# Issuing the last two parts of product P6 together in the two w2·h blocks

## The chip, the cores and the metric

The kernel runs on one core of one Trainium2 chip. That core has four compute engines with queues of their own: TensorE (PE in the profile; its weight loads are listed apart as PEld), VectorE (DVE), ScalarE (ACT) and GpSimd (POOL). SyncE (SP) issues most of the DMA transfers. Within one queue the instructions of this kernel stand in a fixed order, and the queues meet through semaphores. The metric is device time in microseconds, the median of three runs.

## What is computed

With x of 2048 rows by 512 columns, the reference is

```python
g = sigmoid((x * gate_w).sum(-1, keepdims=True))
a = Cr @ (x @ Dr.T) - Ci @ (x @ Di.T)      # the real part of a Fourier transform over both axes
b = (silu(x @ w1) * (x @ w3)) @ w2         # 512 -> 1376 -> 512
out = g * a + (1 - g) * b
```

All arrays are float32. Only the product of h = silu(x w1) · (x w3) with w2 is touched by the change.

## The kernel before

Every large product is done as one step of a Strassen-like scheme with seven products of half-size blocks (P1 to P7), and every operand is split into a high and a low part of type fp32r, so that one logical product becomes three matmuls (`mm3`, L122 by way of `matmul`: high·high, high·low, low·high). The right operand is split while the kernel runs: ACT copies the high part (`high`, L108) and DVE subtracts it from the source to get the low part (`low`, L111). The split pair is called `zo`.

After the gate and up projections (the first 206 us) the work is a list `STEPS` of steps, in blocks. Four blocks of kind "F" multiply by the Fourier matrix of the sequence, two blocks of kind "H" (numbers 4 and 5) compute w2·h, and two of kind "Y" finish the transform over the columns. A step is one *part* q of one product k of a block: part q takes a slice of the contraction. In an H block each product has three parts: q = 0 and q = 1 bring 1024 columns of z (two groups of 512, so 2 × 3 = 6 matmuls into each half of the result, 12 in all), and q = 2 brings 512 (3 into each half, 6 in all). The result of a product has two halves, r = 0 and r = 1, of 128 rows each; each has its own PSUM bank, `ps[0]` and `ps[1]`. A matmul takes 128x128 weights and a 128x512 z.

In H blocks the products stand in the order P1, P5, P6, P7, P3, P2, P4. P1, P6, P7 and P4 share the two banks called X: P6 adds onto what P1 left, and P7 adds onto P6. P5 and P3 share the banks Z. Between P6 and P7 the sum in X must be copied out, as `u2` (`zu` in the profile): when P6's last part has been issued, `read("u2")` puts two ACT copies into ACT's queue (L1061), the first of `ps[0]`, the second of `ps[1]`, each 128x512. P7's first matmul writes into `ps[0]` and so has to wait for the first copy.

One step does, in this order of the program: take its split pair `zt` out of `ZT`, issue its matmuls, `free(zt)`, then `advance(m)`, and after the last part of a product the reads of its banks. `advance(m)` prepares the future: it starts loads (`load_c`), forms a sum for the step four ahead (`sum_c`, on DVE), and splits the operand of the step three ahead (`split_c(m + LEAD)`, `LEAD` = 3). So when P6's part 2 is issued, `advance` splits P7's part 2, and its ACT copy stands in ACT's queue *ahead* of the two copies of X. This is the sequence in ACT's queue around the end of P6, in both kernels: split of P7's part 0 (1024 columns), of P7's part 1 (1024), of P7's part 2 (512), then copy of X's first half, copy of X's second half, then the split of P3's part 0.

The split pairs live in four buffers, the list `ZO`. It is a plain queue: `take` pops the first free one, `free` appends to the end.

```python
def take(places, shape, dtype, name):      # L90
    p, tag = at = places.pop(0)
...
def free(*tiles):                          # L102
    for t in tiles:
        _, places, at = HELD.pop(id(t))
        places.append(at)
```

A new tile in a buffer waits until the last reader of the buffer's former tile is done. With four buffers, a lead of three and one pair freed at each step, there is one free buffer ahead of a step; the split in step m takes the buffer that step m − 1 gave back.

The list `LAST` and the test `m >= len(STEPS) - 2` are there already for the very last two steps of the kernel, whose matmuls are issued together.

Of the kernel before, what the change touches and what calls it, by code (L numbers as in the profile page):

```python
# [32 lines left out]
def fnet_swiglu_gate_kernel(  # L33
# [46 lines left out]
    def bank(k, name):  # L80
        return psum.tile([P, 512], F32, tag=f"ps{k}", name=name)
# [17 lines left out]
    def parts(name):  # L99
        return take(ZO, [P, 2, 4, 256], F32R, name)  # L100
# [5 lines that stand above are left out]
# [36 lines left out]
    def flat(ap):  # L142
        return ap.rearrange("p a n -> p (a n)")
# [300 lines left out]
    zt = parts("b12"), parts("a21")  # L444
# [195 lines left out]
    n = NI - 1 - LOOK  # L640
# [23 lines left out]
    NQ = [{"F": NG // 2, "H": NP2 // 2, "Y": KD // 2}[k] for k in KIND]  # L664
    LEFT_AT = "P3", 0
    STEPS = []
# [32 lines left out]
    def cols(blk, q, form):  # L699

        return 512 if KIND[blk] == "H" and q == NQ[blk] - 1 else 1024
# [80 lines left out]
    def advance(m):  # L782
        load_c(m + LEAD + AHEAD)
        sum_c(m + LEAD + 1)
        split_c(m + LEAD)
# [122 lines left out]
    def spill(blk, k, t, ps=None):  # L908

        src = [t[:, r] for r in range(2)] if ps is None else ps
        if KIND[blk] != "Y":
            g = GT[blk][k // 2] if KIND[blk] == "H" else GT[blk][0]
            for r in range(2):
                nc.vector.tensor_mul(t[:, r], src[r], g)
            if KIND[blk] == "F":
                return nc.gpsimd.dma_start(z_rows(blk, k), flat(t))
            return nc.gpsimd.dma_start(out_part(nbsp, 2 * (blk - NTB) + k // 2, k), t)
        nb, o = other.pop((blk, k))  # L920
        b = nb.rearrange("p (r n) -> p r n", r=2)
        if ps is None:
            nc.vector.tensor_add(flat(t), flat(t), nb)
            nc.sync.dma_start(o, t)
        else:
            last = blk == NB - 1
            for r in range(2 - last):
                nc.vector.tensor_add(t[:, r], ps[r], b[:, r])  # L928
                (nc.scalar if r else nc.sync).dma_start(o[:, r], t[:, r])
            if last:  # L930


                nc.vector.tensor_add(t[:, 1, :256], FINAL[1][:, :256], b[:, 1, :256])
                nc.scalar.dma_start(o[:, 1, :256], t[:, 1, :256])
                nc.scalar.activation(t[:, 1, 256:], ps[1][:, 256:], AF.Copy)  # L935
                nc.sync.dma_start(o[:, 1, 256:], t[:, 1, 256:])
        free(nb)

    GT, other, LAST, FINAL = {}, {}, [], {}

    def out_part(v, tb, k):
        rows = slice(k % 2 * 2 * P, (k % 2 + 1) * 2 * P)
# [33 lines left out]
    def left_step(m):  # L976


        blk = STEPS[m][0]
        w, e = STAT["L"], RL.pop((blk, "e"))  # L980
        z = ZT[m].rearrange("p h a n -> p h (a n)")
        U["P2"] = [bank(b, f"P2_{blk}_{r}") for r, b in enumerate(YB)]
        U["L"] = [bank(b, f"L_{blk}_{r}") for r, b in enumerate(XB[1 - blk % 2])]
        into = [(j, g, ps) for j, names in ((1, ("P5", "L")), (0, ("P2", "P1")))
                for g, ps in enumerate(U[names[0]] + U[names[1]])]
        for n in range(2):
            for j, g, ps in into:
                b = 512 * n + (256, 384, 0, 128)[g]
                matmul(ps, w[:, b : b + P], z[:, j, 512 * n : 512 * n + 512],
                       start=n == 0 and (j, g // 2) in ((0, 0), (1, 1)), stop=False,  # L990
                       skip_group_check=True)
        for j, g, ps in into:
            rows = slice(32 * g, 32 * g + 32)
            matmul(ps, w[rows, 8 * P :], e[rows, 512 * j : 512 * j + 512],
                   start=False, stop=(j, g // 2) == (1, 1), skip_group_check=True)
        free(e)

    def step(m):
        blk, q, k, form = STEPS[m]
        kind = KIND[blk]  # L1000
        if k == "L":
            left_step(m)
            free(ZT.pop(m))
            advance(m)
            for r in range(2):
                nc.vector.tensor_add(U["p5"][:, r], U["p5"][:, r], U["L"][r])
            return spill(blk, 3, U["p5"])
        if q == 0 and k == "P6" and kind != "Y":
            load_gate(blk)
        if blk == NB - 1 and k == "P7" and q == 0:  # L1010
            nb = other[blk, RESULT[k]][0]
            nc.vector.tensor_add(flat(U["p5"]), flat(U["p5"]), nb)
            free(nb)
        own = k in ("P1", "P5", "P2") and (k, kind) != ("P2", "H")
        if q == 0 and own:
            banks = {"P1": XB[blk % 2], "P5": ZB, "P2": YB}[k]
            U[k] = [bank(b, f"{k}_{blk}_{r}") for r, b in enumerate(banks)]
        ps = U[{"P6": "P1", "P7": "P1", "P4": "P1", "P3": "P5"}.get(k, k)]
        zt = ZT.pop(m)
        z = zt.rearrange("p h a n -> p h (a n)")  # L1020
        first = k in ("P1", "P5", "P6", "P3")
        ws = STAT[kind][0 if first else 1]
        steps = [(q, z)]
        if m >= len(STEPS) - 2:
            LAST.append((q, z))
            steps = LAST if m == len(STEPS) - 1 else []
        ni = cols(blk, q, form) // 512
        f = FORMS[kind][k]
        final = blk == NB - 1 and k == "P4"
        if final and steps:  # L1030
            FINAL[1] = bank(XB[1 - blk % 2][0], "P4left")

        def banks_of(r):

            if r == 0 or not final:
                return [(ps[r], slice(None), own)]
            return [(FINAL[1][:, :256], slice(0, 128), True), (ps[1][:, 256:], slice(128, 256), False)]

        for r in range(2):
            sl = slice(r * P, (r + 1) * P)  # L1040
            for dst, some, new in banks_of(r) if steps else ():
                for n, zn in steps:
                    for i in range(ni):
                        w = ws[2 * n + i]
                        b = slice(i * 512, (i + 1) * 512)
                        mm3(dst, w[:, 0, f, sl], w[:, 1, f, sl], zn[:, 0, b], zn[:, 1, b],
                            new and n == 0 and i == 0, n == NQ[blk] - 1 and i == ni - 1, not new,
                            some)
        free(zt)
        advance(m)  # L1050
        if q < NQ[blk] - 1:
            return

        def res(name):
            U[name] = ut.tile([P, 2, 512], F32, tag=name, name=f"z{name}_{blk}")
            return U[name]

        def read(name):
            res(name)
            for r in range(2):  # L1060
                nc.scalar.activation(U[name][:, r], ps[r], AF.Copy)  # L1061

        def plus(name):
            for r in range(2):
                nc.vector.tensor_add(U[name][:, r], U[name][:, r], ps[r])

        if k == "P1":
            read("s1")
        elif k == "P5":
            read("p5")  # L1070
        elif k == "P6":
            read("u2")
        elif k == "P3":
            def result():
                plus("u2")
                spill(blk, 2, U["u2"])

            result() if blk else todo.setdefault(m + 3, []).append((result, ()))
        elif k == "P7" and blk == NB - 1:
            o = other.pop((blk, RESULT[k]))[1]  # L1080
            nb = other[blk, RESULT["P4"]][0].rearrange("p (r n) -> p r n", r=2)
            p5, u3 = U["p5"], res("u3")
            nc.scalar.activation(u3[:, 0], ps[0], AF.Copy)
            for r, v in enumerate((u3[:, 0], ps[1])):
                nc.vector.tensor_add(p5[:, r], p5[:, r], v)
                nc.sync.dma_start(o[:, r], p5[:, r])
            nc.vector.tensor_add(nb[:, 1, :256], nb[:, 1, :256], ps[1][:, :256])
            nc.vector.tensor_add(ps[1][:, 256:], ps[1][:, 256:], nb[:, 1, 256:])
        elif k == "P7":
            read("u3")  # L1090
            nc.vector.tensor_add(flat(U["p5"]), flat(U["p5"]), flat(U["u3"]))
            if kind != "H":
                spill(blk, 3, U["p5"])
        elif k == "P2":
            plus("s1")
            spill(blk, 0, U["s1"])
        else:
            spill(blk, 1, res("c21"), ps)
# [23 lines left out]
    for i, (src, sp, p) in enumerate(late):  # L1122
        blk, b = 1 + i // 3, i % 3
        n = (10, 17, 24)[b]
# [97 lines left out]
```

## Time and profile before

| | us |
|---|---|
| median of 3 runs (lowest, highest) | 674.75 (674.49, 674.79) |
| the profiled execution's own time | 674.51 |
| its span in the trace | 672.7 |
| PE busy in the span | 667.9 |
| DVE busy | 597.0 |
| ACT busy | 374.0 |
| end of P6 in block 4, on the trace's time axis | about 516 |
| end of P6 in block 5 | about 566 |

Times in the trace count from the start of the span. In a timeline each row is a run of like instructions: start, length, engine, line, operation, output<-input, the form, the count, and in brackets how long the engine was idle before it and what ended that. Weight loads (PEld) run ahead of the matmul that they belong to, so a wait of TensorE shows at the weight load. `P` is a bank of a product, `zo` a split pair, `H` the weights from w2, `B` a raw operand.

### The profile page before, as it was taken

To read this page: it belongs to the slowest core of one execution; us is meant where nothing else is said; L and a number is where in the kernel's file an instruction comes from. 1 tells how busy PE (TensorE), PEld (TensorE's weight loads), DVE (VectorE), ACT (ScalarE), POOL (GpSimd) and SP (SyncE) were. 2 spreads that over 40 slices of the span, in tenths; PEclk is the share of its full clock that TensorE was granted. 3 is DMA by queue.
4 is the path that set the end of the run, shared out by engine and by line. 5 is a ranking of instruction groups with operands and counts; after the bars stand their busy time and mean duration, and the time that the engine had idled before them with its cause. 6 is when DMAs were issued, how large, how long until landed. Compare 5 with 4: busy or idle time off the path is not lost.

```text
span 672.7 us, 8720 instructions
## 1 busy us (share of the span) xinstructions
PE 667.9 (99%) x3101; PEld 580.2 (86%) x3101; DVE 597.0 (89%) x749; ACT 374.0 (56%) x505; POOL 66.4 (10%) x123
## 2 busy tenths in 40 slices
PE   9999999999999999999999999999999999999998
PEld 6888888888888888888888888888888888888887
DVE  6999988887679999988899899979797797898996
ACT  6775666655447764466454653654445446455451
POOL 0022112221110000001310101100000010000000
PEclk9999999999999999999999999999999999999999
DMA  7576557499998666815776279919986894784942
GB/s 281 206 296 249 224 205 267 187 340 380 405 418 328 234 216 211 308 64 196 275 263 255 81 248 343 386 41 349 341 323 184 288 347 134 286 313 153 342 130 94
DMA packets 46845, 171.37 MB, mean 255 GB/s; under 512 B 5649, under 2 KB 6225, under 8 KB 43089
## 3 DMA queue, kind: packets, MB, share of 16 engines
q1 hardware_dynamic: 33888, 118.18, 49.7%
q0 software_dynamic: 12624, 52.25, 19.8%
q8 instruction: 24, 0.39, 0.2%
q10 hardware_dynamic: 288, 0.39, 0.2%
q14 instruction: 21, 0.16, 0.1%
HBM read 114.88 MB, written 55.91 MB: 254 GB/s over the span
## 4 chain that ended last, share of the span: by engine, by line
PE 98%; DMA 1%; ACT 0%; DVE 0%; SPq 0%; issue 0%
PE P L122 68%; PE X L122 16%; PE Z L122 8%; PE Y L122 4%; PE C L122 2%; DMA xs_B<-xt 1%; DMA out<-zc 0%; PE L L122 0%; DVE zc L928 0%; ACT xo L108 0%; SPq L242 0%; ACT zc L935 0%
## 5 line engine op out<-in xcount | busy, mean ns | idle before, releaser
L122 PE MATMUL P<-zo,a 128*128 128x512 f32 x1344 | 290.3, 379 | 0.0
L122 PEld LDWEIGHTS P<-zo,a 128*128 128x128 f32 x1344 | 253.9, 189 | 36.3 <-DVE zo L111 0.2
L108 ACT ACTIVATE zo<-B 128x1024 fp32r<-128x1024 f32 (+1 forms) x182 | 185.1, 1022 | 178.5 <-PE P L122 81.1
L111 DVE TENSOR_TENSOR zo<-B,zo 128x1024 fp32r<-128x1024 f32 (+1 forms) x182 | 213.1, 1179 | 26.6 <-ACT zo L108 26.1
L122 PE MATMUL P<-zo,H 128*128 128x512 f32 x420 | 91.9, 380 | 0.1
L751 DVE TENSOR_TENSOR B<-B,B 128x1024 f32<-128x1024 f32 (+1 forms) x78 | 91.8, 1177 | 0.1
L122 PEld LDWEIGHTS P<-zo,H 128*128 128x128 f32 x420 | 79.1, 189 | 12.6 <-ACT zu L1061 0.9
L122 PE MATMUL X<-xo,wb 128*128 128x512 f32 x378 | 88.8, 379 | 0.0
L122 PEld LDWEIGHTS X<-xo,wb 128*128 128x128 f32 x378 | 71.3, 189 | 10.4 <-DMA wb<-wbsp 0.3
L122 PE MATMUL P<-zo,Y 128*128 128x512 f32 (+1 forms) x336 | 71.6, 375 | 0.0
L122 PEld LDWEIGHTS P<-zo,Y 128*128 128x128 f32 x336 | 62.7, 189 | 8.7
L348 POOL DMA_DIRECT2D hsp<-h x40 | 21.7, 543 | 101.5 <-DVE h L408 70.6
L122 PE MATMUL X<-xo,wa 128*128 128x512 f32 x126 | 30.6, 379 | 0.0
L122 PE MATMUL Y<-xo,wa 128*128 128x512 f32 x126 | 30.6, 379 | 0.0
L122 PE MATMUL Z<-xo,wb 128*128 128x512 f32 x126 | 30.6, 379 | 0.0
L122 PE MATMUL Z<-xo,wa 128*128 128x512 f32 x126 | 30.6, 379 | 0.0
L755 DVE TENSOR_TENSOR B<-B,B 128x1024 f32<-128x1024 f32 (+1 forms) x26 | 30.6, 1177 | 0.0
L122 PEld LDWEIGHTS X<-xo,wa 128*128 128x128 f32 x126 | 23.8, 189 | 3.4
L122 PEld LDWEIGHTS Y<-xo,wa 128*128 128x128 f32 x126 | 23.8, 189 | 3.4
L122 PEld LDWEIGHTS Z<-xo,wb 128*128 128x128 f32 x126 | 23.8, 189 | 3.4
L122 PEld LDWEIGHTS Z<-xo,wa 128*128 128x128 f32 x126 | 23.8, 189 | 3.4
L111 DVE TENSOR_TENSOR wa<-ws,wa 128x768 fp32r<-128x768 f32 (+1 forms) x22 | 19.3, 880 | 6.6 <-ACT wa L108 6.4
(166 smaller groups left out, 578.0 us busy)
## 6 DMA issues: line engine op xcount, KB each, us to landing
B<-cc SPq DMA_DIRECT2D x64, 512.0 KB, 5.5
hsp<-h POOLq DMA_DIRECT2D x40, 256.0 KB, 4.1
wbsp<-wb POOLq DMA_DIRECT2D x8, 1024.0 KB, 4.2
wb<-wbsp SPq DMA_DIRECT2D x8, 1024.0 KB, 8.1
B<-hsp SPq DMA_DIRECT2D x16, 512.0 KB, 4.9
B<-zsp SPq DMA_DIRECT2D x16, 512.0 KB, 6.9
ws<-w SPq DMA_DIRECT2D x11, 512.0 KB, 4.7
H<-w2sp SPq DMA_DIRECT2D x5, 1024.0 KB, 8.9
```

The lines of the kernel that those rows point to most:

```text
L108: nc.scalar.activation(hi, src, AF.Copy)
L111: nc.vector.tensor_sub(lo, src, hi.bitcast(F32))
L122: nc.tensor.matmul(ps.rearrange("p (n a) -> p n a", a=2), u, turns(v)[:, some], **kw)
L348: nc.gpsimd.dma_start(hsp[g, b + k, j // 2, :, j % 2 * 512 : (j % 2 + 1) * 512], h)
L751: nc.vector.tensor_add(t, t, RAW[blk, b, q][:, :n])
L755: nc.vector.tensor_sub(t, RAW[blk, "B12", q][:, :n], t)
```

## The change

In the two H blocks, the last two parts of P6 (q = 1 and q = 2) are no longer issued one after the other. At part 1 nothing is issued to TensorE; the pair is put into `LAST` and, as `zt`, into the new list `WAITS`, so that its buffer is not given back yet. `advance` is still called. At part 2 the matmuls of both parts are issued: first all that go into X's first half (6 of part 1, 3 of part 2), then all that go into its second half (6 and 3). Then both buffers are given back, part 2's first and part 1's behind it.

```diff
-    GT, other, LAST, FINAL = {}, {}, [], {}
+    GT, other, LAST, WAITS, FINAL = {}, {}, [], [], {}
...
         steps = [(q, z)]
-        if m >= len(STEPS) - 2:
+        together = m >= len(STEPS) - 2 or (kind, k) == ("H", "P6") and q >= NQ[blk] - 2
+        if together:
             LAST.append((q, z))
-            steps = LAST if m == len(STEPS) - 1 else []
-        ni = cols(blk, q, form) // 512
+            steps = LAST if q == NQ[blk] - 1 else []
...
                 for n, zn in steps:
+                    ni = cols(blk, n, form) // 512
                     for i in range(ni):
...
-        free(zt)
+        if steps:
+            free(zt, *WAITS)
+            LAST.clear()
+            WAITS.clear()
+        else:
+            WAITS.append(zt)
         advance(m)
```

The number of matmuls, copies, splits and transfers is unchanged on every engine.

## The prediction

> **What bounds the kernel now.** I read the page first, then TensorE's list of waits, then the timelines of TensorE and ACT around the two ends of P6.
>
> ```profile
> span 672.7 us, 8720 instructions
> ...
> PE 667.9 (99%) x3101; PEld 580.2 (86%) x3101; DVE 597.0 (89%) x749; ACT 374.0 (56%) x505; POOL 66.4 (10%) x123
> ...
> PE 98%; DMA 1%; ACT 0%; DVE 0%; SPq 0%; issue 0%
> ```
>
> TensorE is busy nearly all the time and is 98% of the chain that ended last. So what is lost on TensorE is lost in the whole, and what any other engine loses counts only where TensorE then waits for it.
>
> ```profile
> PEld P L122 <- issue: 1.3, 4, 0.3
> PEld P L122 <- ACT zu L1061: 0.9, 2, 0.4
> ...
> PEld P L122 <- DVE zo L111: 0.2, 1, 0.2
> ```
>
> These are all the waits of TensorE in the blocks (total us, times, longest). The middle row is the place of the change: two waits, one per H block, of P7's first weight load for the ACT copy of X. The other rows are also the whole reserve: a later TensorE cannot win back more than 0.2 us from DVE, and the issue waits are nobody's. The same from close by, for block 4; first TensorE's steps:
>
> ```profile
> 529.89 30.48 PE L122 MATMUL P<-zo,H 128*128 128x512 f32 x140
> 514.61 0.59 PE L122 MATMUL P<-zo,H 128*128 128x512 f32 x2
> 515.25 0.59 PE L122 MATMUL P<-zo,H 128*128 128x512 f32 x2
> 515.90 0.59 PE L122 MATMUL P<-zo,H 128*128 128x512 f32 x2
> 516.54 0.70 PE L122 MATMUL P<-zo,H 128*128 128x512 f32 x2
> 516.53 0.19 PEld L122 LDWEIGHTS P<-zo,H 128*128 128x128 f32 x1 [0.44 <-ACT zu L1061]
> ```
>
> A matmul lasts 0.38 us, so a row of two that covers 0.59 has its second start at start + 0.59 − 0.38. The first row gives the step from one matmul to the next: (30.48 − 0.38) / 139 = 0.2165 us. In the second row the second matmul, at 514.82, is the last of P6's part 1; six of part 2 follow: three into X's first half (last start 515.46), three into its second (last start 516.11). P7's weight load then comes at 516.53 with 0.44 idle before it. Its second matmul starts at 516.54 + 0.70 − 0.38 = 516.86, where without a wait it would be at 516.11 + 2 × 0.2165 = 516.54: the wait costs 0.32 us net, twice, 0.64 us in all. That is everything there is to gain here.
>
> ```profile
> 515.29 0.63 ACT L108 ACTIVATE zo<-B 128x512 fp32r<-128x512 f32 x1 [1.53 <-PE P L122]
> 515.89 0.60 ACT L1061 ACTIVATE zu<-P 128x512 f32<-128x512 f32 x1
> 516.53 0.60 ACT L1061 ACTIVATE zu<-P 128x512 f32<-128x512 f32 x1
> ```
>
> The first row is the split of P7's part 2, ahead of the copies in ACT's queue. It waits for TensorE: its buffer was that of P6's part 1, whose last matmul started at 514.82, so it starts 0.47 later, still beside part 2's matmuls. The first copy starts 0.43 after its own last matmul (515.46), the second 0.42 after its own (516.11). So now the split delays the copy hardly at all.
>
> **The change, part by part.** *The matmuls.* The same 18 of parts 1 and 2 in another order; TensorE has as many steps, cost nothing. Part 2's operand is wanted six steps (1.3 us) earlier. P6's last matmul starts at 516.11 and part 1 begins 17 steps before, at 512.43; with the change part 2 begins six steps later, at 513.73. In block 5 all is 49.92 us later (last start 566.03, below), so 563.65. The low halves of these operands end at 510.28 and 561.26:
>
> ```profile
> 509.59 0.69 DVE L111 TENSOR_TENSOR zo<-B,zo 128x512 fp32r<-128x512 f32 x1
> 560.58 0.68 DVE L111 TENSOR_TENSOR zo<-B,zo 128x512 fp32r<-128x512 f32 x1
> ```
>
> Over 2 us in hand: nothing lost. By itself the new order would do good: X's first half would be complete nine matmuls before the second instead of three, so its copy could run beside them.
>
> *The buffers.* But part 1's pair is no longer given back at part 1, and at part 2 `free(zt, *WAITS)` appends part 2's buffer first, part 1's second. `advance` comes right behind and its split of P7's part 2 pops the first: **the buffer of P6's part 2, whose last reader is now P6's very last matmul**. Before, it was part 1's. Nothing else is free at that point: of four buffers two hold P7's parts 0 and 1. The waits in ACT's queue, read from the two built programs (S is the number of P6's last matmul in TensorE's count):
>
> ```
>              before                     after
> split P7/2   TensorE >= S-6             TensorE >= S
> copy X, 1st  TensorE >= S-3             none of TensorE
> copy X, 2nd  TensorE >= S               none of TensorE
> ```
>
> The copies need no wait of their own any more because they stand behind the split. So in place of "copy beside the second half's matmuls" comes a chain in series: last matmul, split, copy, P7's weight load.
>
> *Its price.* Last matmul to split: 0.47, by the present split. Split to copy: where one 512-wide ACT instruction follows another and waits for nothing, the start to start is 0.53 (522.60 to 523.13):
>
> ```profile
> 519.48 0.63 ACT L733 ACTIVATE zo<-left_a 128x512 fp32r<-128x512 f32 x1 [1.41 <-issue]
> 520.13 0.63 ACT L733 ACTIVATE zo<-left_b 32x512 fp32r<-32x512 f32 x1
> ...
> 522.60 0.63 ACT L733 ACTIVATE left_e<-left_c 128x512 fp32r<-128x512 f32 x1
> 523.13 1.04 ACT L108 ACTIVATE zo<-B 128x1024 fp32r<-128x1024 f32 x1
> 524.08 0.57 ACT L1061 ACTIVATE zu<-P 128x512 f32<-128x512 f32 x1
> 524.08 1.06 ACT L1061 ACTIVATE zu<-P 128x512 f32<-128x512 f32 x2
> ```
>
> Copy to weight load: 516.53 − 515.89 = 0.64. So the load comes at 516.11 + 0.47 + 0.53 + 0.64 = 517.75 instead of 516.53: **1.22 us later**. What follows the wait is as before, so this is the loss. In block 5:
>
> ```profile
> 565.21 0.63 ACT L108 ACTIVATE zo<-B 128x512 fp32r<-128x512 f32 x1 [1.53 <-PE P L122]
> 565.82 0.59 PE L122 MATMUL P<-zo,H 128*128 128x512 f32 x2
> 566.45 0.19 PEld L122 LDWEIGHTS P<-zo,H 128*128 128x128 f32 x1 [0.44 <-ACT zu L1061]
> ```
>
> last matmul 566.03, split at 566.50, copy at 567.03, load at 567.67 against 566.45: 1.22 again. Bounds of one block: 0.42 (a copy's lag behind its matmul), 0.49 (two `zu`, 0.57 the first, 1.06 together) and 0.62 (such a shorter copy, with the same 0.05 from its end to the load) give 1.53 and a loss of 1.11; 0.47, 0.65 (519.48 to 520.13, with a wait for a transfer between) and 0.65 give 1.77 and a loss of 1.35. I take 1.22 since its rows are nearest: same sizes, same line, no other wait.
>
> *The second copy* starts half a microsecond behind the first, at 517.6, and ends at 518.2; P7's first matmul into X's second half comes six steps after the load, at 519.0: covered, by 0.8 us.
>
> *Who else waits.* Behind the split stands DVE's low half of the same operand (now at 515.95, then some 1.3 us later, by 517.9); DVE's queue has nothing else to do then, its next row waits for ACT:
>
> ```profile
> 515.95 0.69 DVE L111 TENSOR_TENSOR zo<-B,zo 128x512 fp32r<-128x512 f32 x1 [0.94 <-ACT zo L108]
> 517.03 1.05 ACT L108 ACTIVATE zo<-B 128x1024 fp32r<-128x1024 f32 x1
> 568.02 1.23 DVE L111 TENSOR_TENSOR zo<-B,zo 128x1024 fp32r<-128x1024 f32 x1 [1.47 <-ACT zo L108]
> ```
>
> P7's part 2 is wanted 24 steps (5.2 us) after P7 begins, near 523: covered. The split of P3's part 0 (517.03) moves to some 518.2, wanted at P7's end, 30 steps after its start. Everything later on ACT and DVE moves with TensorE by the same 1.2 us. SP and POOL issue the same transfers in the same order; those that wait for nothing here come as early as before, which can only help. From the two stalls on, TensorE has no reserve but the 0.2 us named.
>
> *The clock.* Idle time of the weight loads becomes 0.44 + 1.22 = 1.66 us in each block. The nearest stall in the trace is at the head, 1.30, and the granted clock there is full:
>
> ```profile
> core 0: us, PE busy (x) PEld busy (x) DVE busy (x) ACT busy (x) POOL busy (x), PEclk, DMA share, GB/s
> 4.50:6.50 2.00, 1.20 (x6) 0.78 (x5) 1.38 (x3) 1.14 (x3) 0.00 (x0) 1.00 0.98 383
> 0.78 3.85 PE L434 MATMUL wps<-const-bfloat16-1.0 128*128 128x512 bf16 x11 [0.78 <-PEq L1211]
> 5.43 0.30 PEld L122 LDWEIGHTS C<-xo,wa 128*128 128x128 f32 x2 [1.30 <-ACT xo L108]
> ```
>
> So I add nothing for it. [...]
>
> *The sum.* 2 × 1.22 = 2.44 us, bounds 2.22 and 2.70. On the profiled execution's 674.51 that is 676.95; that run lies 0.24 below the median of the three (674.75), on which it would be 677.19. I say **677.1 us**, +0.35%.
>
> **The rivals.** *1. The split does not hold the copies back*, so the order does what the words of the change say. X's first half is then complete nine steps before the end, the copy starts at 516.11 − 9 × 0.2165 + 0.43 = 514.59, ends at 515.2, and the wait is gone: −0.64 us, 674.1 (−0.09%). It decides where the split starts by 516.12 − 0.64 − 0.53 = 514.95, so where its buffer's last reader starts by 514.48, eight matmuls before the last one. For it: the wait of 0.4 is real. Against it: the buffer's reader is the last matmul. Chance 0.04.
>
> *2. The wait is for part 1's matmuls only* (buffer order the other way round). Part 1's last matmul would be three from the end, at 515.46; split 515.93, copy 516.46, load 517.10: 0.57 later, 1.14 in all, 675.8 (+0.16%). For it: before, it was part 1's buffer; against it: `free` appends part 2's first. Chance 0.04.
>
> *3. The clock falls after the longer stalls.* The only slow matmuls of the trace are the eleven at the head, (3.85 − 0.38) / 10 = 0.35 a step. If each stall is followed by eleven such steps, 11 × (0.35 − 0.2165) = 1.5 us more per block: 680.1 (+0.8%). For it: the stall is longer than any in the trace; against it: full clock after 1.30. Chance 0.04.
>
> **How the numbers follow.** Forecast 0.88, rivals 0.04 each. The forecast's own range, bounds of the sum on either base, is 676.7 to 677.45. A measurement of this kernel tells about 0.2% (1.35 us, so 673.4 to 676.1) from no change. Of both signs only rival 1 lies below; more than eight in ten lie with the forecast, so the range is its own with a little for the medians' scatter of 0.3 between runs: 676.5 to 677.6. Slower: forecast and rival 3, 0.92; same: rivals 1 and 2, 0.07 and a bit; faster, 0.01.
>
> **What would show it.** Right: TensorE's waits for `zu` L1061 go from 0.9 to some 3.3 us, still two; ACT's `zo` 128x512 at the end of P6 begins about 0.47 behind P6's last matmul and both `zu` follow it without a gap, the first 0.5 later; TensorE's busy steps keep 0.2165 us. Wrong: a first copy that starts before the last matmul of P6 (rivals 1 and 2), a PEclk digit below 9 in the slices near 516 or 567 (rival 3), or a wait for DVE or a DMA that grows in blocks 5 to 7, which would say that the delay does not shift everything alike.

## The result, and the profile after

| | before | changed |
|---|---|---|
| median, us (6 runs each) | 674.79 (674.49 to 675.07) | 677.24 (676.87 to 677.73) |
| profiled execution, its own time | 674.51 | 677.14 |
| span in the trace | 672.7 | 675.4 |
| waits of TensorE for `zu`, us | 0.9 | 3.3 |

The ratio is 1.0036, with a 95% interval of 1.0023 to 1.0049: slower by 2.45 us. The forecast was 677.1 (676.5 to 677.6).

TensorE's waits in the changed kernel, from its list of waits (weight loads; total us, times, longest; the copy of X now has line 1067):

```profile
PEld P L122 <- ACT zu L1067: 3.3, 2, 1.7
...
PEld P L122 <- issue: 1.3, 4, 0.3
...
PEld P L122 <- DVE zo L111: 0.2, 1, 0.2
```

Still two waits, of 1.66 us each instead of 0.44; the other two rows are what they were. The end of P6 in block 4 of the changed kernel, in the timelines of TensorE and ACT (start us, length us):

```profile
516.01 0.59 PE L122 MATMUL P<-zo,H 128*128 128x512 f32 x2
517.85 0.19 PEld L122 LDWEIGHTS P<-zo,H 128*128 128x128 f32 x1 [1.66 <-ACT zu L1067]
517.86 0.70 PE L122 MATMUL P<-zo,H 128*128 128x512 f32 x2 [1.25 <-ACT zu L1067]
...
516.69 0.63 ACT L108 ACTIVATE zo<-B 128x512 fp32r<-128x512 f32 x1 [2.83 <-PE P L122]
517.22 0.58 ACT L1067 ACTIVATE zu<-P 128x512 f32<-128x512 f32 x1
517.22 1.07 ACT L1067 ACTIVATE zu<-P 128x512 f32<-128x512 f32 x2
```

P6's last matmul starts at 516.01 + 0.59 − 0.38 = 516.22. Then the four links stand one behind the other: the split 0.47 later (516.69), the first copy 0.53 after the split (517.22), the weight load 0.63 after the copy (517.85). The split's bracket says that ACT had been idle for 2.83 us, waiting for TensorE: the copy of X's first half, complete nine steps earlier, stood behind it all that time. In block 5 it is the same:

```profile
567.82 0.63 ACT L108 ACTIVATE zo<-B 128x512 fp32r<-128x512 f32 x1 [2.83 <-PE P L122]
568.36 1.06 ACT L1067 ACTIVATE zu<-P 128x512 f32<-128x512 f32 x2
568.99 0.19 PEld L122 LDWEIGHTS P<-zo,H 128*128 128x128 f32 x1 [1.66 <-ACT zu L1067]
```

Nothing is won back or lost further on. TensorE's busy time by stages, first of the changed kernel, then of the one before (length of the stretch, busy us):

```profile
496.00:530.00 34.00, 32.75 (x152) 28.38 (x151) 24.93 (x27) 19.40 (x27) 0.53 (x1) 1.00 0.71 241
530.00:600.00 70.00, 68.75 (x327) 58.88 (x327) 60.63 (x73) 33.64 (x43) 5.04 (x7) 1.00 0.74 260
600.00:660.00 60.00, 60.00 (x280) 52.55 (x279) 57.03 (x55) 32.65 (x39) 0.72 (x1) 1.00 0.63 223
```

```profile
496.00:530.00 34.00, 33.96 (x162) 28.90 (x162) 25.05 (x28) 20.18 (x28) 0.53 (x1) 1.00 0.76 262
530.00:600.00 70.00, 69.96 (x328) 60.44 (x329) 62.96 (x75) 34.56 (x44) 5.05 (x7) 1.00 0.76 266
600.00:660.00 60.00, 60.00 (x280) 52.54 (x279) 57.05 (x56) 32.45 (x39) 0.72 (x1) 1.00 0.59 210
```

One block's stall lies in each of the first two stretches, 1.2 us of busy time is missing in each, and behind them TensorE is full again, at a granted clock of 1.00 throughout. The spans differ by 2.7, not 2.4: 0.1 is there before block 4 (516.22 against 516.11), in the head of the kernel, and the rest behind the last matmul; neither touches the change.

### The profile page after: what moved, and what is told of

It is laid out like the page before. It is cut to its first block, busy times and chain, and to the rows that moved or that the text cites. A ratio compares the mean times of both kernels' runs of the same rounds, so it can differ in the third digit from the quotient of the medians.

```text
span 675.4 us, 8714 instructions
## 1 busy us (share of the span) xinstructions
PE 668.4 (99%) x3101; PEld 580.7 (86%) x3101; DVE 596.7 (88%) x749; ACT 373.2 (55%) x505; POOL 66.4 (10%) x123
```

## The experiments

Theory: part 2's buffer, given back first, makes the split of P7's part 2 wait for P6's last matmul, and the copies of X are late because they stand behind that split in ACT's queue. Rivals: the new order of the matmuls costs the time by itself; or the late buffer does, wherever the copies stand.

**The hold alone.** The kernel before, its own order of matmuls, with the buffers given back as in the change:

```diff
-    GT, other, LAST, FINAL = {}, {}, [], {}
+    GT, other, LAST, WAITS, FINAL = {}, {}, [], [], {}
...
-        free(zt)
+        if (kind, k) == ("H", "P6") and q == NQ[blk] - 2:
+            WAITS.append(zt)
+        else:
+            free(zt, *WAITS)
+            WAITS.clear()
         advance(m)
```

> The kernel before with its own order of matmuls, but part 1's buffer is given back only after part 2's, as in the change. Theory (the buffer alone makes the loss): the same last matmul, split, copy, load in series, so 677.2, waits for zu 3.3 us. Rival (the order of the matmuls makes it): 674.8, waits 0.9.

Measured 677.13 us (8 runs), ratio 1.0029 (1.0019 to 1.0039) to 674.79. From its list of waits, and from its timelines at the end of P6 in block 4:

```profile
PEld P L122 <- ACT zu L1065: 3.3, 2, 1.7
...
516.67 0.63 ACT L108 ACTIVATE zo<-B 128x512 fp32r<-128x512 f32 x1 [2.83 <-PE P L122]
517.21 1.07 ACT L1065 ACTIVATE zu<-P 128x512 f32<-128x512 f32 x2
...
517.84 3.32 PEld L122 LDWEIGHTS P<-zo,H 128*128 128x128 f32 x16 [1.66 <-ACT zu L1065]
```

It is the same chain, link by link. The whole loss is there without a single matmul moved. What changed the time is not what the change's words speak of, the order of the matmuls, but when and in which order two buffers are given back.

**The other buffer.** The changed kernel with part 1's buffer given back first:

```diff
-            free(zt, *WAITS)
+            free(*WAITS, zt)
```

> The changed kernel, but part 1's buffer is given back ahead of part 2's, so that the split of P7's part 2 takes part 1's buffer and waits for part 1's last matmul, three steps (0.65 us) before P6's end. Theory (the chain last reader, split, copy, weight load sets the wait): the load comes 0.65 us earlier than in the changed kernel in each block, so 1.3 us in all: 677.24 - 1.3 = 675.9, with the waits for zu at about 2.0 us in all instead of 3.3. Rival (the loss comes from the new order of the matmuls, not from the buffer): stays at 677.2.

Measured 675.73 us (12 runs, one of which took 678.53 at a mean granted clock of 1.000), ratio 1.0016 (1.0006 to 1.0026). Its waits and its ACT timeline at the end of P6 in block 4:

```profile
PEld P L122 <- ACT zu L1067: 2.0, 2, 1.0
```

```profile
516.32 0.63 ACT L108 ACTIVATE zo<-B 128x512 fp32r<-128x512 f32 x1 [2.18 <-PE P L122]
516.86 1.06 ACT L1067 ACTIVATE zu<-P 128x512 f32<-128x512 f32 x2
```

The last matmul that the split waits for comes three steps earlier, the split's idle time falls from 2.83 to 2.18, by 0.65 = three steps, and the wait falls with it from 1.66 to 1.01. The wait follows the split's start, step for step. Part 1's last matmul still lies so near P6's end that the copies stay late, so this order too loses time, only less.

**The copies first.** The changed kernel, buffers and matmuls as changed, with the two copies put ahead of the split in ACT's queue:

```diff
-        advance(m)
+        late = (kind, k) == ("H", "P6") and q == NQ[blk] - 1
+        if not late:
+            advance(m)
...
             read("u2")
+            if late:
+                advance(m)
```

> The changed kernel, but at P6's last part the two copies of X are put into ACT's queue ahead of the split of P7's part 2; buffers and matmuls as changed. Theory (the split loses the time only because the copies stand behind it in ACT's queue): the first copy starts nine matmuls before P6's end, TensorE does not wait at all: 674.79 - 0.64 = 674.15, waits for zu 0. Rival (order of the matmuls, or the late buffer itself, costs): 676 to 677.2. Second rival (the late split is then missed by P7's part 2 or by DVE): a wait of TensorE for zo by DVE or ACT of over 0.5 us.

Measured 673.90 us (12 runs), ratio 0.9985 (0.9976 to 0.9993): 0.89 us faster than before and 3.3 faster than the changed kernel. It is the best of all kernels tried. In its list of waits no row for `zu` is left; these are all that TensorE has in the blocks:

```profile
PEld P L122 <- issue: 1.3, 4, 0.3
PEld P L122 <- DVE zo L111: 0.2, 1, 0.2
```

Its ACT timeline at the end of P6 in block 4 (this execution took 676.19 us, the 11 others 673.64 to 674.44; in it TensorE's weight loads at the head came to their full pace late, from 10.55 us on, so all times are some 2 us later; the last section has more on that):

```profile
516.73 0.60 ACT L1069 ACTIVATE zu<-P 128x512 f32<-128x512 f32 x1 [0.83 <-PE P L122]
518.68 0.60 ACT L1069 ACTIVATE zu<-P 128x512 f32<-128x512 f32 x1 [1.35 <-PE P L122]
519.17 1.57 ACT L108 ACTIVATE zo<-B 128x512 fp32r<-128x512 f32 x2
```

The copies are 1.95 us apart, nine steps of 0.2165: each follows its own half at once. The split now comes last, with the same late buffer as in the change, and nobody waits for it. So the late buffer by itself costs nothing that these runs can tell; what costs is that the split which waits for it stands ahead of the copies.

**The copies first, in the kernel before.** The same edit without the new order and without the hold.

> The kernel before, its order of matmuls and its buffers, with only the two copies of X put ahead of the split of P7's part 2. Theory (before, the first copy was bound by its own last matmul, 0.43 behind it, and the split ahead of it cost nothing): the two waits of 0.44 stay, 674.8. Rival (the split ahead of the copies already cost time before the change, so that the gain of 0.9 us with the changed order comes from the queue alone): 673.9, waits gone.

Measured 674.73 us (11 runs) against 674.72, ratio 1.0000 (0.9991 to 1.0009). The wait stands:

```profile
PEld P L122 <- ACT zu L1063: 0.9, 2, 0.4
```

So the gain above needs both: the new order of matmuls, and the copies ahead of the split. The first without the second is the change, a loss; the second without the first gives nothing.

**One block only.** The change in block 4, not in block 5:

```diff
-        together = m >= len(STEPS) - 2 or (kind, k) == ("H", "P6") and q >= NQ[blk] - 2
+        together = m >= len(STEPS) - 2 or (blk, k) == (NTB, "P6") and q >= NQ[blk] - 2
```

> The change in block 4 only. Theory (each block adds its own 1.22 us, nothing given back later): 674.79 + 1.22 = 676.0, one wait for zu of 1.66 and one of 0.44, 2.1 us in all. Rival (a delay in the first block is partly won back, or makes the second worse): under 675.5 or over 676.5.

Measured 676.06 us (12 runs), ratio 1.0018 (1.0007 to 1.0029), waits for `zu` 2.1 us in two, the longest 1.7. Each block pays its own 1.2. One of the 12 runs took 678.69 us, at a mean granted clock of 0.997 where the others have 0.999 or 1.000; no trace of it was kept, and the clock is taken up below.

**More in the chain.** The changed kernel, with ACT's copy of that split done twice:

```diff
             high(t[:, 0, :n], src[:, :n])
+            if KIND[blk] == "H" and (k, q) == ("P7", NQ[blk] - 1):
+                high(t[:, 0, :n], src[:, :n])
```

> The changed kernel, with the ACT copy of the split of P7's part 2 done twice in both H blocks (the same values written again). Theory (what stands in ACT's queue between P6's last matmul and the copy of X is paid in full by TensorE): one more 128x512 copy per block, 0.53 us, or up to 0.75 if the second waits for the first to be written: 677.24 + 1.1 to 1.5 = 678.3 to 678.7, waits for zu 4.4 to 4.8 us. Rival (part of the loss is a fixed cost of the semaphores and the extra copy hides in it): 677.2 to 677.7.

Run beside the changed kernel itself:

> The changed kernel once more, on the same chip as the two others of this set, as their base: 677.2, waits for zu 3.3 us. No theory expects another time.

The changed kernel took 677.60 (5 runs, ratio 1.0042, 1.0029 to 1.0055). With the copy doubled the waits grew from 3.3 to 4.6 us, 0.65 per block and copy, inside what was expected (0.53 by a row, up to 0.75 by an estimate that no run shows), and two of six runs took 678.1 and 678.2. But the median was 680.0 (ratio 1.0072, 1.0060 to 1.0083): the other four took 679.9 to 680.7, at a mean granted clock of 0.997. That was a miss: the median lies 1.3 us above the upper end of what was expected. Two more profiled executions of the same kernel, and a kernel with the copy done four times (a loop of three in place of the `if`), were to tell where the 2 us between the two groups of runs lie:

> The kernel with the split's copy done twice, one more look, to see where the 2 us lie that four of its six runs took above the profiled one (678.1). Theory A: 678.1, or more with slow first matmuls at the head of the kernel. Theory B: near 680, with matmul steps of 0.3 us or more behind the stall in block 4 or 5.

> A second such look at the kernel with the split's copy done twice. Theory A: 678.1, or more with slow first matmuls at the head of the kernel. Theory B: near 680, with matmul steps of 0.3 us or more behind the stall in block 4 or 5.

> The changed kernel with the ACT copy of the split of P7's part 2 done four times in both H blocks (the same values). One extra copy lengthened each of the two waits by 0.65 us. Theory A (the stall alone is paid, 0.65 us per copy and block, and the scatter up to 680.7 in the timed runs with one extra copy comes from the head of the kernel): 677.4 + 6 x 0.65 = 681.3, waits for zu 7.2 us, every matmul after the stalls 0.2165 us behind the one before, and a granted clock of 1.00 there. Theory B (a stall this long lets TensorE's clock fall for a while in some runs): some 2 us more per block in which it falls, 683 to 686, with steps of 0.3 us or more behind a stall and a granted clock under 1.00 in that stretch.

The two executions took 679.96 and 680.15 us. With four copies the median was 684.31 (4 runs, ratio 1.0131, 1.0114 to 1.0148), the waits 7.3 us. All three show theory B. In the execution at 679.96, TensorE around the stall of block 4 (weight loads and matmuls with their wait; then by stretches: length, busy time and count of PE, PEld, DVE, ACT, POOL, granted clock, DMA share, GB/s):

```profile
518.29 4.73 PEld L122 LDWEIGHTS P<-zo,H 128*128 128x128 f32 x15 [2.32 <-ACT zu L1069]
518.30 0.92 PE L122 MATMUL P<-zo,H 128*128 128x512 f32 x3 [1.92 <-ACT zu L1069]
```

```profile
516.27:519.68 3.41, 1.49 (x7) 1.24 (x7) 0.69 (x1) 3.18 (x5) 0.00 (x0) 1.00 0.20 65
519.70:523.08 3.38, 3.38 (x9) 2.70 (x8) 1.23 (x1) 0.58 (x1) 0.00 (x0) 0.50 0.32 107
523.10:526.50 3.40, 3.40 (x17) 2.99 (x16) 1.38 (x2) 3.32 (x7) 0.00 (x0) 1.00 0.13 51
```

Some 1.4 us after TensorE has resumed, the granted clock is 0.50 in the row of 3.38 us from 519.70 to 523.08; in the rows on both sides of it, to 519.68 and from 523.10, it is 1.00. The lowered row has nine matmuls, where the next has 17; its eight weight loads start from 519.70 on and the next one at 523.11, 0.43 us apart. The matmuls after the stalls of blocks 4 and 5 (to 528 and to 580 us), first in the execution at 678.11, then at 679.96, then at 680.15:

```profile
518.21 9.33 PE L122 MATMUL P<-zo,H 128*128 128x512 f32 x42 [1.92 <-ACT zu L1069]
570.00 9.33 PE L122 MATMUL P<-zo,H 128*128 128x512 f32 x42 [1.92 <-ACT zu L1069]
...
518.30 9.94 PE L122 MATMUL P<-zo,H 128*128 128x512 f32 x37 [1.92 <-ACT zu L1069]
571.78 8.47 PE L122 MATMUL P<-zo,H 128*128 128x512 f32 x38 [1.92 <-ACT zu L1069]
...
518.59 9.72 PE L122 MATMUL P<-zo,H 128*128 128x512 f32 x36 [1.92 <-ACT zu L1069]
572.07 8.25 PE L122 MATMUL P<-zo,H 128*128 128x512 f32 x37 [1.91 <-ACT zu L1069]
```

The idle time before them is the same in all six rows. The mean step, (9.33 − 0.38) / 41 = 0.218 us, is the full pace in four of them and 0.27 us in two, those of block 4 in the executions at 679.96 and 680.15. With four copies the execution profiled had a mean granted clock of 0.995, and the steps were long behind both stalls: 28 matmuls in 8.00 us in block 4 and 15 in 5.19 in block 5, 0.28 and 0.34 us each.

## Why the prediction was right, step by step

- *TensorE is the bound, and what it loses the whole loses.* It held: 2 × (1.66 − 0.44) = 2.44 us of longer weight-load waits, 2.45 us in the medians.
- *The buffer.* The split took part 2's buffer and waited for P6's last matmul: the bracket of 2.83 in the changed kernel, and 675.73 with the buffers the other way round. Rival 2, priced at 1.14 us, was the price of that other order, and the run gave 0.94 (0.4 to 1.75 by the interval). The sign that the prediction named for it, a first copy ahead of P6's last matmul, was not its sign: by the prediction's own sum that copy comes at 516.46, behind 516.11, and in the run it came at 516.86, behind 516.51. What tells the two orders apart is the split's idle time, 2.18 against 2.83.
- *The price.* Predicted links 0.47, 0.53 and 0.64, measured 0.47, 0.53 and 0.63. For the second link it had rows of 0.49, 0.53 and 0.65 to choose from, and its reason for 0.53, "same sizes, same line", was not right: the row is a copy of L733 followed by a 128x1024 split, neither the split and the copy of X nor the same size behind. What the row shares with the link is its first instruction, 0.63 us long, and no other wait between the two. With the copy doubled each further copy of the same tile took 0.65 us more; why the link is longer there no run shows.
- *What would be covered* was: no wait of TensorE for a second copy, for P7's part 2 or for P3's part 0 appeared.
- *Rival 1* (the copies not held back, −0.64) did not happen in the change but is the run with the copies first: −0.89, with an interval of −0.5 to −1.6 that holds the −0.64.
- *Rival 3, the clock,* did not happen in any of the 11 runs of the changed kernel; the granted clock was 1.00. But it lay nearer than its chance of 0.04 let one think: with 0.67 us more idle time it came in six of eight runs (a mean granted clock of 0.997). The run of 678.69 us with the change in block 4 only has that mean too, so there the clock may have fallen without longer idle time. The prediction set the waits of the weight loads side by side, 1.66 against 1.30 at the head; the matmuls themselves were idle for 1.25 and 0.80. Its price, 1.5 us, came from a misread row: of the eleven matmuls at the head, "0.35 a step", the first seven stand some 0.43 apart, up to the one at 3.29 us, and the rest 0.22 to 0.30. What one fall cost was eight steps at 0.43, 1.7 us: from P6's last matmul in block 4 to that in block 5 it is 53.48 us in the execution at 679.96 and 51.79 in that at 678.11.

The range held because the wait, the path and each link could be read from rows of the trace of before. That the forecast of 677.1 lies 0.14 us from the median is partly luck: the second set of runs of the changed kernel gave 677.60, on the upper edge of the range.

## What to carry to other kernels

An edit to the order of matmuls can move nothing and still cost: look where it gives buffers back, which waiting instruction that puts into which queue, and what stands behind it there. A copy out of PSUM that TensorE waits for belongs ahead of work for later steps in its engine's queue; in the changed kernel that alone turned +0.36% into −0.15%, though in the kernel before, where the split did not hold the copy back, it gave nothing. The price of such a chain could be read in advance, link by link, from rows of like shape: matmul start to split start, start to start of two ACT instructions, copy start to weight load.

## What the runs showed of the hardware

The granted clock of TensorE was lower after some of the longer idle times, and the length of the idle time alone does not decide it. A wait of the weight loads of 1.66 us, which is what the change makes (the matmuls are idle for 1.25 us in it), was not followed by a lower clock in any profiled execution: seven such waits in four traces, with a mean granted clock of 1.000 in each. One of 2.32 us (1.92 of the matmuls) was in two cases of six, block 4 of the executions at 679.96 and 680.15, with a mean of 0.997. One of 3.6 us (3.24 of the matmuls) was in both blocks of the one trace that has it, with a mean of 0.995.

Why the same wait was followed by a lower clock in one execution and not in another, no run shows. The run of 678.69 us stays open too. Its mean of 0.997 is that of the executions at 679.96 and 680.15, and in the one trace of its kernel the longest wait for `zu` is 1.7 us; where its clock fell, no trace shows.

The matmuls at the head of the kernel are slow at first as well. In the kernel before, their weight loads are 0.43 us apart up to the one at 3.29 us, the step of the lowered stretch above; the four from there take 0.84 us, about half of that each, and from 6.86 us on six loads take 1.30 us, 0.217 each:

```profile
2.44 0.15 PEld L434 LDWEIGHTS <-const-bfloat16-1.0 128*128 128x128 bf16 x1 [0.28 <-issue]
2.86 0.15 PEld L434 LDWEIGHTS <-const-bfloat16-1.0 128*128 128x128 bf16 x1 [0.28 <-issue]
3.29 0.84 PEld L434 LDWEIGHTS <-const-bfloat16-1.0 128*128 128x128 bf16 x4 [0.28 <-issue]
...
6.86 1.27 PEld L122 LDWEIGHTS C<-xo,a 128*128 128x128 f32 x6
8.16 0.41 PEld L122 LDWEIGHTS C<-xo,wa 128*128 128x128 f32 x2
```

How long the slow pace lasts differs between executions of like kernels. In the one with the copies first that took 676.19 us, 2.3 us longer than that kernel's median, the six loads from 8.61 us on still take 1.94 us, 0.32 each, and 0.216 is the step from 10.55 on:

```profile
8.61 1.92 PEld L122 LDWEIGHTS C<-xo,a 128*128 128x128 f32 x6
10.55 2.56 PEld L122 LDWEIGHTS C<-xo,wa 128*128 128x128 f32 x12
13.14 1.27 PEld L122 LDWEIGHTS C<-b,wa 128*128 128x128 f32 x6
```

The loads of its last row begin at 10.84 us in the kernel before, 2.3 us earlier.
